# A one-core kernel for local attention and two feed-forward blocks: a new price list for its instruction scheduler, a cheaper mask table, and P·V of two quads in one run

## The chip, the core and the metric

The kernel runs on one NeuronCore of a Trainium2 chip (trn2). A core has five engines with a queue of instructions each: TensorE (PE in the profile, its weight loads PEld), VectorE (DVE), ScalarE (ACT), GpSimd (POOL) and SyncE (SP, which here only issues transfers). Each engine runs its own queue in order, and semaphores hold an instruction back until what it needs is there. PE writes its results to PSUM, which has 8 banks of 128 x 512 fp32 words; all else lies in SBUF. The metric is the device time of one execution in microseconds, the median of several.

## The reference, cut to what matters

```python
# q, k, v: (2, 8, 768, 64) fp32; n_global = 8, n_local = 96
scores = (q @ k.T) / sqrt(64)
keep   = (key < n_global) | ((rel >= 0) & (rel < n_local))      # rel = query - key
dist   = where(global and not local, n_local, abs(rel))
scores = where(keep, scores - slope[head] * dist, -1e9)         # slope[h] = 2 ** -(h + 1)
a      = exp(scores - max) / (sum + 1e-9)
x      = (a @ v) as 1536 tokens x 512
h = x @ w_in        # (512 x 2048)
x = where(h >= 1, h, where(h <= -1, 0, (h + 1) ** 2 / 4)) @ w_out
h = x @ w_in2
out = maximum(0.01 * h, h) @ w_out2                             # 1536 x 512
```

The four weight matrices come as 64-bit floats.

## The kernel before, in words

All products but the transposes and P·V are made in fp32r: each operand is split into a high part and a low rest, and three products (high x high, high x low, low x high) are added up in PSUM.

**Attention.** The 1536 queries are 12 tiles of 128 (`Tt`, `t` its place in its batch of 6), the heads two quads of four, so there are 24 quads (`quad`). A quad sees its own 128 keys and the 128 before them, whose first 32 columns are overwritten by the batch's first 32 keys. Its steps are: load K and Q (`ld`, SP); four transposes into one bank (`tr`, L559, PE); high and low parts of both (`ev_hi`, `ev_lo`, by ACT or DVE); twelve score matmuls (`s_mm`, L591, PE), which use 64 rows of the array each, two at a time; a DVE operation that adds the mask table `b8` and takes the row maximum (`mx`, L600); the exponential with its sum (`ex`, L609, ACT); reciprocal (`rs`, DVE); normalisation (`nm`, L622 on DVE or L624 on POOL); eight transposes of P into two banks (`p_tr`, L633, PE); their evacuation into a buffer `pT` (`p_ev`, ACT or DVE), of which there are two; eight matmuls by V (`x_mm`, L646, PE; sixteen rows in the trace), which use 64 columns of the array each; high and low parts of the result into `x`.

**The mask table.** `b8` has 8 heads x 512 columns. It is made in the first microseconds: POOL writes distances (`c_iota`), DVE or POOL cuts them off at `n_local` (`c_table`, three operations for each of two stretches of columns, 128 and 384), then each head's slope is multiplied in (`c_heads`, sixteen operations, on DVE, ACT and POOL). `n_local` and `n_global` come by two tiny transfers from SP's queue, and a matmul (L387) spreads them over the partitions.

**Feed-forward.** The first block works on 256 tokens at a time for its first two of 16 hidden chunks (matmuls of 128 x 256, woven into the attention), and on 512 at a time for the rest (`hid` L727, `mm` L789, 128 x 512). The second block makes seven products for two groups of 512 tokens instead of eight (`two`: L921, L988, L1003). Each weight chunk of 128 x 512 (64 of them) is loaded as 64-bit words (SP) and turned to fp32 high and low parts in eight steps on ACT, DVE and POOL (`job`: L438 to L465). The last step adds PSUM to `part` and sends it out (L846, L849).

**The order** on every engine is worked out at build time by `Schedule.run`: a list scheduler that goes through the program in modelled time. Each operation has a cost for each engine that may run it and a priority, which is a due time from the tables at L1064 to L1073. An engine that falls free takes the ready operation with the lowest priority whose buffers (rings of tiles: banks, `pT`, `raw` and so on) are free. A consumer on another engine is ready `HOP` = 200 ns after its producer's end. VectorE operations that read no PSUM and POOL operations are not placed at the same modelled time. While the first four quads are not through, PE runs a dummy matmul (L369) wherever the model has it idle.

```python
same = [u for u in o.users if not o.tail and len(u.costs) == 1 and e in u.costs]
heapq.heappush(events, (end, k, e, same))
heapq.heappush(events, (end + o.tail + (0 if e == NONE else self.HOP), k + 0.5, e, (o, [...])))
```

Of the kernel before, what the change touches and what calls it, by code (L numbers as in the profile page):

```python
# [8 lines left out]
F32 = mybir.dt.float32  # L9
# [8 lines left out]
P = 128  # L18
G = 32
# [13 lines left out]
KDN, VDN, QTN, SMN, PTN, GN, RAWN, WDN, WRN = 3, 3, 3, 3, 2, 4, 4, 2, 2  # L33
# [18 lines left out]
class Op:  # L52
    __slots__ = ("costs", "fn", "prio", "takes", "gives", "waits", "users", "at", "done", "tail", "ps")


class Schedule:

    HOP = 200  # L60

    SLOW = 7000.0
# [7 lines left out]
    def add(self, costs, fn, prio, after=(), takes=(), gives=(), tail=0.0, ps=False):  # L70
# [4 lines left out]
        o.costs, o.fn, o.prio, o.gives, o.tail, o.ps = costs, fn, prio, gives, tail, ps  # L75
# [11 lines left out]
    def run(self):  # L87
        ready = [[] for _ in range(6)]
        events = []
        n = 0  # L90
        now = 0.0
        busy = [0.0] * 6

        held = 0.0
        left = len(self.ops)

        def enter(o):
            nonlocal n
            for e in o.costs:
                heapq.heappush(ready[e], (o.prio, n, o))  # L100
                n += 1

# [3 lines left out]
        k = 0  # L106
        while left:
            started = True
            while started:
                started = False  # L110
                for e in range(6):
                    if busy[e] > now:
                        continue
                    kept = []
                    got = None
                    while ready[e]:
                        x = heapq.heappop(ready[e])
                        o = x[2]
                        if o.done is not None:
                            continue  # L120
                        if e == DVE and not o.ps and busy[POOL] > now or e == POOL and held > now:
                            kept.append(x)
                            if len(kept) > 40:
                                break
                            continue
                        if all(len(s.ring.free) > y for s, y in o.takes):
                            got = o
                            break
                        kept.append(x)
                        if len(kept) > 40:  # L130
                            break
                    for x in kept:
                        heapq.heappush(ready[e], x)
                    if got is None:
                        if e == PE and self.fill and self.fill[0].done is not None and self.fill[0].done <= now:
                            self.fill[1]()
                            busy[e] = now + FILLN / (1.2 if now < self.SLOW else 2.4)
                            k += 1
                            heapq.heappush(events, (busy[e], k, e, None))
                        continue  # L140
                    started = True
                    o = got
                    for s, _ in o.takes:
                        s.tile = s.ring.free.pop(0)
                    end = now + o.costs[e] * (2 if e == PE and now < self.SLOW else 1)
                    o.done = end
                    o.at = now
                    busy[e] = end
# [4 lines left out]
                    k += 1  # L153

                    same = [u for u in o.users if not o.tail and len(u.costs) == 1 and e in u.costs]
                    heapq.heappush(events, (end, k, e, same))
                    heapq.heappush(events, (end + o.tail + (0 if e == NONE else self.HOP), k + 0.5, e, (o, [u for u in o.users if u not in same])))
# [3 lines left out]
            now = events[0][0]  # L161
            while events and events[0][0] <= now:
                users = heapq.heappop(events)[3]
                if users is None:
                    continue
                if isinstance(users, tuple):
                    o, users = users
                    for s in o.gives:
                        s.ring.free.append(s.tile)
                for u in users:  # L170
# [1046 lines left out]
```

## Time and profile before

| | us |
|---|---|
| median of 3 runs | 617.87 (617.7 to 618.28) |
| the profiled execution, first to last instruction (span) | 615.8 |
| PE busy in it | 607.2 (99%) |
| DVE, ACT, POOL busy | 474.5, 354.4, 204.9 |
| last matmul starts | 608.4 (its group of three) |

The profiled execution's span is 615.8 us, 2.0 us under the median of the runs; the runs also hold what lies before the first and behind the last instruction. PE's rows give a start that is recorded and an end that is modelled, and each matmul's row overlaps the next, so what a run of matmuls takes is read from its start to the start of the run behind it. Dummy matmuls count as busy.

### The profile page before, as it was taken

The numbers are of one execution on the slowest core, as the hardware profiler recorded it, in microseconds if no ns is written. First come the engines' busy times: TensorE is split into PE (matmuls) and PEld (weight loads), VectorE is DVE, ScalarE is ACT, GpSimd is POOL, SyncE is SP. The second block draws the span as 40 slices with busy tenths as digits, with TensorE's granted clock in tenths as the row PEclk, the third lists the DMA queues.
The fourth block names the chain that finished last, engine by engine and source line by source line (L and its number), as shares of the span: only waits on it lengthen the run. The fifth ranks groups of instructions, "written<-read, shape, count | busy, mean of one in ns | idle before, by whom it ended". The sixth has DMA issues, their size and how long they took to land.

```text
span 615.8 us, 9602 instructions
## 1 busy us (share of the span) xinstructions
PE 607.2 (99%) x3408; PEld 507.2 (82%) x3408; DVE 474.5 (77%) x1036; ACT 354.4 (58%) x762; POOL 204.9 (33%) x248
## 2 busy tenths in 40 slices
PE   8999999999999999999999999999999999999995
PEld 7879888898888888888888888888888888888884
DVE  6999999989983779923469998736988966988563
ACT  6999889767764446734436476524465634464300
POOL 3556576632320102300104152202646422546200
PEclk9999999999999999999999999999999999999998
DMA  9846433124330314300002013200232320220014
GB/s 192 207 104 177 136 89 87 53 65 158 121 110 28 102 35 136 107 32 1 0 11 92 5 65 101 72 1 1 68 106 68 101 69 1 68 70 1 2 65 146
DMA packets 61809, 46.98 MB, mean 76 GB/s; under 512 B 39608, under 2 KB 56248, under 8 KB 61752
## 3 DMA queue, kind: packets, MB, share of 16 engines
q1 hardware_dynamic: 61752, 46.28, 25.8%
q8 instruction: 29, 0.48, 0.4%
q14 instruction: 28, 0.23, 0.1%
HBM read 43.12 MB, written 3.15 MB: 75 GB/s over the span
## 4 chain that ended last, share of the span: by engine, by line


## 5 line engine op out<-in xcount | busy, mean ns | idle before, releaser
L789 PE MATMUL bank<-g,w 128*128 128x512 f32 (+1 forms) x648 | 141.3, 367 | 0.0
L727 PE MATMUL bank<-x,w 128*128 128x512 f32 (+1 forms) x648 | 140.6, 367 | 0.0
L789 PEld LDWEIGHTS bank<-g,w 128*128 128x128 f32 x648 | 112.6, 188 | 20.5 <-issue 0.7
L727 PEld LDWEIGHTS bank<-x,w 128*128 128x128 f32 x648 | 112.3, 188 | 20.1 <-issue 0.3
L828 DVE TENSOR_TENSOR part<-bank,part 128x512 f32<-128x512 f32 x96 | 63.6, 686 | 27.3 <-PE bank L1003 23.2
L1003 PE MATMUL bank<-w,g 128*128 128x512 f32 x312 | 80.9, 389 | 0.0
L1003 PE MATMUL bank<-w,w 128*128 128x512 f32 x264 | 70.1, 389 | 0.0
L459 POOL TENSOR_TENSOR wd<-wd,wr 128x512 int32<-128x512 int32 x33 | 44.9, 1362 | 72.0 <-DVE wd L452 67.6
L1003 PEld LDWEIGHTS bank<-w,g 128*128 128x128 f32 x312 | 58.6, 188 | 12.2
L220 ACT CAST g<-t 128x512 fp32r<-128x512 f32 (+1 forms) x73 | 42.6, 585 | 41.2 <-PE bank L789 20.6
L220 ACT CAST w<-wd 128x512 fp32r<-128x512 f32 x61 | 37.8, 620 | 45.0 <-DVE wd L459 13.4
L734 ACT ACTIVATE t<-bank,half 128x512 f32<-128x512 f32 (+1 forms) x54 | 34.3, 638 | 47.1 <-PE bank L727 42.6
L228 POOL TENSOR_TENSOR w<-wd,w 128x512 fp32r<-128x512 f32 x32 | 42.5, 1332 | 52.3 <-ACT w L220 48.3
L1003 PEld LDWEIGHTS bank<-w,w 128*128 128x128 f32 x264 | 49.6, 188 | 10.3
L749 DVE SCALAR_TENSOR_TENSOR t<-bank,t 128x512 f32<-128x512 f32 (+1 forms) x54 | 33.9, 628 | 28.7 <-ACT t L742 28.1
L444 POOL TENSOR_SCALAR wd<-wd 128x512 f32<-128x512 f32 x26 | 17.5, 673 | 111.5 <-ACT wd L438 101.1
L452 DVE SCALAR_TENSOR_TENSOR wd<-raw,wd 128x512 int32<-128x512 int32 x64 | 49.5, 774 | 1.7
L226 DVE TENSOR_TENSOR g<-t,g 128x512 fp32r<-128x512 f32 (+1 forms) x54 | 37.0, 692 | 16.5 <-ACT g L220 15.8
L456 ACT ACTIVATE wr<-raw 128x512 int32<-128x512 uint32 x64 | 42.4, 670 | 10.5 <-DVE wd L459 10.1
L921 PE MATMUL bank<-x,w 128*128 128x512 f32 x192 | 47.8, 390 | 0.0
L609 ACT ACTIVATE sm<-sm,st 128x256 f32<-128x256 f32 (+1 forms) x96 | 46.2, 490 | 1.9 <-DVE st L600 1.9
L988 PE MATMUL bank<-x,w 128*128 128x512 f32 x192 | 45.1, 389 | 0.0
(116 smaller groups left out, 953.7 us busy)
## 6 DMA issues: line engine op xcount, KB each, us to landing
raw<-in_moe_w_in_dram SPq DMA_DIRECT2D x32, 512.0 KB, 3.8
raw<-in_moe_w_out_dram SPq DMA_DIRECT2D x32, 512.0 KB, 3.4
kd<-in_k_dram SPq DMA_DIRECT2D x24, 128.0 KB, 3.0
qd<-in_q_dram SPq DMA_DIRECT2D x24, 128.0 KB, 3.5
vd<-in_v_dram SPq DMA_DIRECT2D x12, 256.0 KB, 3.2
out_dram<-part SPq DMA_DIRECT2D x11, 256.0 KB, 3.2
out_dram<-part SPq DMA_DIRECT2D x2, 128.0 KB, 3.4
vg<-in_v_dram SPq DMA_DIRECT2D x2, 64.0 KB, 3.9
```

What stands on the lines that cost most here:

```text
L220: A.copy(out=out_, in_=in_)
L228: GP.tensor_tensor(out=out_, in0=a, in1=b, op=ALU.subtract)
L452: V.scalar_tensor_tensor(out=Dd.tile, in0=hl()[0], scalar=-0x40000000, in1=Dd.tile, op0=ALU.bitwise_and, op1=ALU.bitwise_or)
L456: A.activation(out=Rr.tile, in_=hl()[1], func=AF.Copy, scale=2.0 ** -29)
L459: (V if e == DVE else GP).tensor_tensor(out=Dd.tile, in0=Dd.tile, in1=Rr.tile, op=ALU.add)
L609: A.activation(out=Sm.tile[:, a, 0:W], in_=Sm.tile[:, a, 0:W], func=AF.Exp, scale=-1.0, bias=St.tile[:, 0, a:a + 1], accum_out=St.tile[:, ...
L727: T.matmul(out=Hb.tile[:, 0:n], lhsT=wi.tile[:, a, kk * P:(kk + 1) * P], rhs=x[r][:, b, kk, c0:c0 + n], start=(kk == 0 and a + b == 0), st ...
L789: T.matmul(out=o[:, z * n:(z + 1) * n], lhsT=wo.tile[:, a, cc * P:(cc + 1) * P], rhs=Gt.tile[:, b, 0:n], start=st, stop=sp_)
L828: V.tensor_tensor(out=part[r][sl], in0=ac(), in1=part[r][sl], op=ALU.add)
L921: T.matmul(out=bank.tile, lhsT=w.tile[:, a, (2 * z + kk) * P:(2 * z + kk + 1) * P], rhs=xx()[:, b, kx + kk, :], start=st and kk == 0 and a ...
L988: T.matmul(out=Hb.tile, lhsT=w.tile[:, a, kk * P:(kk + 1) * P], rhs=x[2][:, b, kk, :], start=(kk == 0 and a + b == 0), stop=(kk == KD - 1 ...
L1003: T.matmul(out=Bo.tile, lhsT=Gt[z, r].tile[:, b, cb * P:(cb + 1) * P], rhs=wo[z].tile[:, a, :], start=(z == 0 and a + b == 0), stop=(z == ...
```

## The change

1. **The scheduler's model.** The single `HOP` becomes a latency by the producer's engine, one table for consumers on PE (`LAG_PE`) and one for the others (`LAG`). PE's operations have a kind: plain, transpose, scores (64 rows), P·V (64 columns). A table `TURNS` prices the change from one kind to another, and PE looks through up to twelve ready operations for the lowest sum of priority and ten times that price. Transfers have a size; the model lets them queue behind each other at 4.6 ns for each KB, and an issue is priced at 0.5 us. K and Q of a quad are two operations instead of one. Operations that may run on several engines can have a later due time on one of them (`LATE`). All due times have new values; the old ones stay for the fallback that the shown inputs don't take.
2. **The mask.** `c_far` (POOL, while `n_local` is on its way) makes `far` = distance x 1e30. `c_table` then needs one DVE operation for each stretch: max(far − (n_local − 0.5) x 1e30, distance). The table `tab` has one entry for each pair of heads (4 x 512 columns), eight operations instead of sixteen. The odd head's slope is half of the even head's, so `ev_hi` and `ev_lo` multiply Q by `sc` (1 on the first 64 partitions, 2 on the others), and `mx` scales that head by half as much.
3. **P·V in one run.** `quad` is a generator now, and from tile 3 on (`X2` = 3) the P·V matmuls of a tile's two quads are one operation, made when the second quad comes to it. There is still `PTN` = 2. The rings `sm` and `st` have 4 places instead of 3.
4. **The two tiny transfers** of `n_local` and `n_global` go out from ACT's queue, ahead of its table load.

```diff
+PLAIN, TURN, ROWS, COLS = range(4)
+TURNS = ((0, 50, 125, 165), (-82, 0, 92, 92), (185, 185, 0, 185), (153, 153, 120, 53))
+LAG = (200, 140, 120, 80, 50, 0)
+LAG_PE = (0, 285, 240, 300, 100, 0)
+LOOK = 12
+PER_KB = 4.6
+STICK = 10.0
...
-    HOP = 200
...
+        def pick(e):
...
+                if e != PE:
+                    got = x
+                    break
+                c = x[0] + STICK * TURNS[mode][o.mode]
+                if got is None or c < best:
+                    got, best = x, c
+                seen += 1
+                if seen >= LOOK:
+                    break
...
+                    c = o.costs[e]
+                    if e == PE:
+                        c = c * (2 if now < SLOW else 1) + TURNS[mode][o.mode]
+                        mode = o.mode
+                    end = land = now + c
+                    if o.kb:
+                        busy[e] = max(end, landed - BACKLOG)
+                        land = landed = max(busy[e] + o.tail, landed + o.kb * PER_KB)
...
+    def c_far(e, c0, c1):
+        GP.tensor_scalar(out=far[:, c0:c1], in0=rel[:, c0:c1], scalar1=1.0e30, scalar2=0.0, op0=ALU.mult, op1=ALU.add)
+
     def c_n(e):
         V.tensor_copy(out=n_f, in_=Nb.tile[:, 0:2])
+        V.tensor_scalar(out=cut, in0=Nb.tile[:, 0:1], scalar1=-0.5, scalar2=1.0e30, op0=ALU.add, op1=ALU.mult)
...
     def c_table(e, c0, c1):
-        E = V if e == DVE else GP
-        r, u = rel[:, c0:c1], far[:, c0:c1]
-        E.tensor_scalar(out=u, in0=r, scalar1=nl, scalar2=1.0e30, op0=ALU.is_ge, op1=ALU.mult)
-        E.tensor_tensor(out=r, in0=r, in1=u, op=ALU.add)
+        r = rel[:, c0:c1]
+        V.scalar_tensor_tensor(out=r, in0=far[:, c0:c1], scalar=cut, in1=r, op0=ALU.subtract, op1=ALU.max)
...
-        for h in range(h0, h0 + 4):
-            o, r, f = b8[:, h, c0:c1], rel[:, c0:c1], -8.0 * 2.0 ** (-8.0 * (h + 1) / H)
+        for p in (p0, p0 + 1):
+            o, r, f = tab[:, p, c0:c1], rel[:, c0:c1], -8.0 * 2.0 ** (-8.0 * (2 * p + 1) / H)
...
-                nc.sync.dma_start(out=n_w[0:1, :, z], in_=a.bitcast(I32))
+                A.dma_start(out=n_w[0:1, :, z], in_=a.bitcast(I32))
...
         def ev_lo(e):
-            for z in range(2):
-                sub(e, at(z, 1), two(b1.tile[:, z * 2 * P:(z + 1) * 2 * P]), at(z, 0).bitcast(F32))
+            kk, qq = two(b1.tile[:, 0:2 * P]), two(b1.tile[:, 2 * P:4 * P])
+            sub(e, at(0, 1), kk, at(0, 0).bitcast(F32))
+            V.scalar_tensor_tensor(out=at(1, 1), in0=qq, scalar=sc, in1=at(1, 0).bitcast(F32), op0=ALU.mult, op1=ALU.subtract)
...
-        ob = add({PE: 436 * nb + 100}, x_mm, d + DUE["xmm"], oa + vx, takes=[b4, h4], gives=[Pt] + vs_)
-        vx_op[i] = ob
+        heldx[i] = x_mm, oa + vx, [b4, h4], [Pt] + vs_
+        if Tt >= X2 and not last:
+            yield
+        if Tt < X2 or last:
+            of = [i - 1, i] if Tt >= X2 else [i]
+            ob = add({PE: 436 * nb * len(of)}, lambda e, of=of: [heldx[z][0](e) for z in of], t_att[of[0]] + due_["xmm"], sum((heldx[z][1] for z in of), []),
+                     takes=sum((heldx[z][2] for z in of), []), gives=sum((heldx[z][3] for z in of), []), mode=COLS)
...
+S2, X2 = 99, 3
```

PE's queue, tile 3: the P·V matmuls of its two quads (`pT` is the evacuated P, `vd` are V's rows, `kd` and `qd` the loaded K and Q of a later quad). Before:

```order
L646 MATMUL bank_72<-pT_128,vd_117 64x128 x2
L646 MATMUL bank_72<-pT_128,vd_115 64x128 x2
L646 MATMUL bank_72<-pT_128,vd_117 64x128 x2
L646 MATMUL bank_72<-pT_128,vd_115 64x128 x2
L559 MATMUL bank_73<-ident,kd_111 128x128 x2
L559 MATMUL bank_73<-ident,qd_114 128x128 x2
L646 MATMUL bank_76<-pT_129,vd_117 64x128 x2
L646 MATMUL bank_76<-pT_129,vd_115 64x128 x2
L646 MATMUL bank_76<-pT_129,vd_117 64x128 x2
L646 MATMUL bank_76<-pT_129,vd_115 64x128 x2
```

And now:

```order
L694 MATMUL bank_76<-pT_130,vd_117 64x128 x2
L694 MATMUL bank_76<-pT_130,vd_115 64x128 x2
L694 MATMUL bank_76<-pT_130,vd_117 64x128 x2
L694 MATMUL bank_76<-pT_130,vd_115 64x128 x2
L694 MATMUL bank_77<-pT_131,vd_117 64x128 x2
L694 MATMUL bank_77<-pT_131,vd_115 64x128 x2
L694 MATMUL bank_77<-pT_131,vd_117 64x128 x2
L694 MATMUL bank_77<-pT_131,vd_115 64x128 x2
L602 MATMUL bank_73<-ident,kd_109 128x128 x2
L602 MATMUL bank_73<-ident,qd_112 128x128 x2
```

The transposes of K and Q no longer part the two quads. Over the whole order, PE comes to score matmuls 24 times before and 19 times now, and to P·V 23 times before and 15 times now. Its dummy matmuls are 94 before and 84 now; 41 of them stood ahead of the first score matmul, now 33. Ahead of the last P·V stood 228 matmuls of 128 x 256 and 24 of 128 x 512; now 216 and none. All other matmuls are the same in number and shape.

DVE's queue, from the copy of `n_local` and `n_global` out of PSUM (`n_f`) to the first quad's low parts (`ks`, `qt`); `t_98` holds the distances. Before:

```order
L343 COPY n_f<-bank_72 128x2
L344 TENSOR_SCALAR gl<-gl,n_f 128x32
L345 TENSOR_SCALAR gl<-gl,n_f 128x32
L350 TENSOR_SCALAR t_99<-t_98,n_f 128x128
L351 TENSOR_TENSOR t_98<-t_98,t_99 128x128
L353 TENSOR_TENSOR t_98<-t_98,gl 128x32
L350 TENSOR_SCALAR t_99<-t_98,n_f 128x384
L351 TENSOR_TENSOR t_98<-t_98,t_99 128x384
L355 COPY t_98<-gl 128x32
L226 TENSOR_TENSOR ks<-bank_71,ks 128x2x128
L226 TENSOR_TENSOR qt_119<-bank_71,qt_119 128x2x128
```

And now:

```order
L381 COPY n_f<-bank_71 128x2
L382 TENSOR_SCALAR cut<-bank_71 128x1
L383 TENSOR_SCALAR gl<-gl,n_f 128x32
L384 TENSOR_SCALAR gl<-gl,n_f 128x32
L388 SCALAR_TENSOR_TENSOR t_98<-t_99,cut,t_98 128x128
L390 TENSOR_TENSOR t_98<-t_98,gl 128x32
L388 SCALAR_TENSOR_TENSOR t_98<-t_99,cut,t_98 128x384
L392 COPY t_98<-gl 128x32
L259 TENSOR_TENSOR ks<-bank_72,ks 128x2x128
L619 SCALAR_TENSOR_TENSOR qt_119<-bank_72,sc,qt_119 128x2x128
```

Two operations are gone and a one-column one has come. Of the operations that write the table, four stood on DVE, eight on ACT and four on POOL; now none, four and four. Ahead of DVE's last attention operation stood 450 operations, now 434; among them 13 evacuations of P of 128 x 512, now 7.

SP's queue from its start. Before:

```order
L656 DMA kd_109<-in_k_dram 128x4x64
L656 DMA qd_112<-in_q_dram 128x4x64
L384 DMA n_w<-in_n_local_dram 1x2x1
L384 DMA n_w<-in_n_global_dram 1x2x1
L656 DMA kd_110<-in_k_dram 128x4x64
L656 DMA qd_113<-in_q_dram 128x4x64
L656 DMA kd_111<-in_k_dram 128x4x64
```

And now:

```order
L703 DMA kd_109<-in_k_dram 128x4x64
L703 DMA qd_112<-in_q_dram 128x4x64
L703 DMA kd_110<-in_k_dram 128x4x64
L703 DMA qd_113<-in_q_dram 128x4x64
L470 DMA raw_78<-in_moe_w_in_dram 128x4x256
L703 DMA kd_111<-in_k_dram 128x4x64
L703 DMA qd_114<-in_q_dram 128x4x64
```

The second quad's K and Q come up by the two tiny transfers, and a weight chunk stands ahead of the third quad's.

## Rows read from the trace of the kernel before

**Rows 1.** The page's head and its busy times.

```profile
span 615.8 us, 9602 instructions
PE 607.2 (99%) x3408; PEld 507.2 (82%) x3408; DVE 474.5 (77%) x1036; ACT 354.4 (58%) x762; POOL 204.9 (33%) x248
```

**Rows 2.** Four stretches: busy us (instructions) of PE, PEld, DVE, ACT, POOL; clock; DMA share, GB/s.

```profile
0.00:4.42 4.42, 3.36 (x18) 2.45 (x19) 0.41 (x6) 1.28 (x1) 2.49 (x15) 1.00 0.28 63
4.42:28.60 24.18, 23.67 (x240) 19.63 (x239) 22.39 (x107) 21.46 (x78) 8.99 (x22) 1.00 0.97 225
28.60:128.00 99.40, 99.05 (x1007) 86.15 (x1005) 93.53 (x339) 88.20 (x275) 59.81 (x97) 1.00 0.41 104
128.00:600.00 472.00, 471.93 (x2111) 391.70 (x2110) 352.87 (x580) 243.45 (x409) 133.61 (x116) 1.00 0.19 60
```

**Rows 3.** The dummy matmuls (L369) alone: PE busy, PEld busy.

```profile
4.42:28.60 24.18, 10.38 (x78) 7.44 (x77) 1.00 0.97 225
```

**Rows 4.** Timeline of PE in the attention: start us, us, instruction, how many.

```profile
42.43 0.97 PE L591 MATMUL bank<-ks,qt 64*128 64x256 f32 x12
43.33 0.65 PE L633 MATMUL bank<-ident,sm 128*128 128x128 f32 x4
43.92 1.09 PE L646 MATMUL bank<-pT,vd 128*64 128x128 f32 x16
44.94 0.44 PE L559 MATMUL bank<-ident,kd 128*128 128x128 f32 x2
...
47.95 0.38 PE L559 MATMUL bank<-ident,kd 128*128 128x128 f32 x2
...
48.39 0.60 PE L633 MATMUL bank<-ident,sm 128*128 128x128 f32 x4
```

**Rows 5.** Timeline of PE where two P·V runs follow each other, and behind.

```profile
87.81 1.97 PE L646 MATMUL bank<-pT,vd 128*64 128x128 f32 x32
89.71 0.98 PE L591 MATMUL bank<-ks,qt 64*128 64x256 f32 x12
...
91.03 1.67 PE L727 MATMUL bank<-x,w 128*128 128x256 f32 x12
92.53 0.60 PE L633 MATMUL bank<-ident,sm 128*128 128x128 f32 x4
```

**Rows 6.** Waits of PE's weight loads: us in total, times, longest us.

```profile
PEld bank L633 <- DVE sm L622: 1.2, 4, 0.4
...
PEld bank L559 <- DMA qd<-in_q_dram: 0.8, 1, 0.8
```

**Rows 7.** Timeline of PE at the only gap behind the attention.

```profile
357.31 1.29 PE L789 MATMUL bank<-g,w 128*128 128x512 f32 x5
358.68 1.20 PE L921 MATMUL bank<-xt,w 128*128 128x512 f32 x4
```

**Rows 8.** Timeline of DVE and POOL, and PE's loads, at a wait of PE.

```profile
36.31 1.72 DVE L622 TENSOR_SCALAR sm<-sm,st 128x256 f32<-128x256 f32 x4
...
36.78 0.61 POOL L444 TENSOR_SCALAR wd<-wd 128x512 f32<-128x512 f32 x1 [2.00 <-ACT wd L438]
37.37 1.00 POOL L624 TENSOR_SCALAR sm<-sm,st 128x256 f32<-128x256 f32 x2
37.59 0.20 PEld L633 LDWEIGHTS bank<-ident,sm 128*128 128x128 f32 x2 [0.44 <-DVE sm L622]
...
39.82 0.59 DVE L622 TENSOR_SCALAR sm<-sm,st 128x256 f32<-128x256 f32 x2
```

**Rows 9.** DVE's groups for the table and the evacuated P: busy us, mean ns.

```profile
L222 DVE COPY pT<-bank 128x512 f32<-128x512 f32 x13 | 8.8, 686 | 1.8 <-PE bank L633 1.8
L364 DVE TENSOR_SCALAR b<-t 128x384 f32<-128x384 f32 x4 | 1.2, 356 | 0.0
L351 DVE TENSOR_TENSOR t<-t,t 128x384 f32<-128x384 f32 x1 | 0.6, 558 | 0.0
L350 DVE TENSOR_SCALAR t<-t,n_f 128x384 f32<-128x384 f32 x1 | 0.4, 416 | 0.0
```

More of the change, by code (lines that the diff above doesn't have):

```diff
@@ L99, in enter, with event @@
             for e in o.costs:
-                heapq.heappush(ready[e], (o.prio, n, o))
+                heapq.heappush(ready[e], (o.prio + o.late.get(e, 0.0), n, o))
                 n += 1
+        def event(at, e, o, kind):
+            nonlocal k
+            k += 1
+            heapq.heappush(events, (at, k, e, o, kind))
+        def pick(e):
+            kept = []
+            got = None
+            best = 0.0
+            seen = 0
+            while ready[e]:
+                x = heapq.heappop(ready[e])
+                o = x[2]
+                if o.done is not None:
+                    continue
+                kept.append(x)
+                if len(kept) > 40:
+                    break
+                if e == DVE and not o.ps and busy[POOL] > now or e == POOL and held > now:
+                    continue
+                if not all(len(s.ring.free) > y for s, y in o.takes):
+                    continue
+                if e != PE:
[6 more added lines that the diff above has]
+                if seen >= LOOK:
+                    break
+            for x in kept:
+                if x is not got:
+                    heapq.heappush(ready[e], x)
+            return got and got[2]
         for o in self.ops:
@@ L105, in run @@
                 enter(o)
-        k = 0
         while left:
@@ L113, in run @@
                         continue
[L114 to L131, printed above, removed]
@@ L152, in run @@
                     left -= 1
[L153 to L157, printed above, removed]
+                    event(end, e, None, 0)
+                    event(land + LAG[e], e, o, 1)
+                    event(land + LAG_PE[e], e, o, 2)
             if not events:
@@ L215, in emit, with LATE @@
     sch = Schedule()
+    def LATE(kind):
+        return {e: due_[kind + "@" + n] for e, n in ((ACT, "A"), (DVE, "V")) if kind + "@" + n in due_}
     add = sch.add
@@ L666, in quad @@
         elif t > 1:
[L667 removed]
+            kv_op[i] = add(fc, first, d + due_["kg"], [s_op[i - NQ], kv_op[i - NQ]], late=LATE("kg"))
         else:
             kv_op[i] = kv_op[i - NQ]
[L670 to L672 removed]
+        held[i] = s_mm, [ol, kv_op[i] if t > 1 else None], b2 + h2 + [Sm, St], [Qt]
@@ new lines, in quad @@
+        if Tt >= S2 and not last:
+            yield
+        if Tt < S2 or last:
+            of = [i - 1, i] if Tt >= S2 else [i]
+            o4 = add({PE: 720 * len(of)}, lambda e, of=of: [held[z][0](e) for z in of], t_att[of[0]] + due_["s"], sum((held[z][1] for z in of), []),
+                     takes=sum((held[z][2] for z in of), []), gives=sum((held[z][3] for z in of), []), mode=ROWS)
+            for z in of:
+                s_op[z] = o4
+            if Tt >= S2:
+                yield
@@ L673, in quad @@
+        o4 = s_op[i]
         o6 = []
         for z in range(2):
-            o5 = add({DVE: 2 * (dve(W) + 10)}, mx(z), d + DUE["mx"] + z, [o4, o_tb[1 if t else 0][pq]], gives=[b2[z], h2[z]], ps=True)
-            o6.append(add({ACT: 2 * (180 + act(W, False))}, ex(z), d + DUE["ex"] + z, [o5]))
-        o7 = add({DVE: 278}, rs, d + DUE["rs"], o6)
-        opt = add({NONE: 0}, lambda e: None, d - 4300, [o7], takes=[Pt])
-        nms = [add({POOL: 2 * (pool_ts(W) + 83), DVE: 2 * (dve(W, True) + 62)}, nm(y), d + DUE["nm"] + y, [o7]) for y in range(2)]
@@ L680, in quad @@
-        o9 = [add({PE: 110 * 2 * nb}, p_tr(y), d + DUE["ptr"] + y, [nms[y], opt], takes=[b3[y], h3[y]])
+            o5 = add({DVE: 2 * (dve(W) + 10)}, mx(z), d + due_["mx"] + z, [o4, o_tb[1 if t else 0][pq]], gives=[b2[z], h2[z]], ps=True)
+            o6.append(add({ACT: 2 * (180 + act(W, False))}, ex(z), d + due_["ex"] + z, [o5]))
+        o7 = add({DVE: 278}, rs, d + due_["rs"], o6)
+        opt = opts[i] = add({NONE: 0}, lambda e: None, d - 4300, [o7, opts.get(i - 1)], takes=[Pt])
+        nms = [add({POOL: 2 * (pool_ts(W) + 83), DVE: 2 * (dve(W, True) + 62)}, nm(y), d + due_["nm"] + y, [o7], late=LATE("nm")) for y in range(2)]
```

221 lines of the change are left out of this document (117 added, 104 removed).

## The prediction

> **What bounds the kernel now.** I began with the head of the page: a span of 615.8 us in which PE is busy for 607.2 [rows 1]. Matmul rows overlap and dummies count, so this alone does not make PE the bound. The stretches of the span say more [rows 2]. From 128 to 600 us PE is busy for 471.93 of 472.00 us while DVE has work for 352.87: behind the attention PE is the only bound, and the one gap that I find there is at 358 us, where five matmuls that take 0.227 each at their usual distance (1.13) are followed only after 1.37 [rows 7], a loss of 0.2. From 28.6 to 128 us PE is busy for 99.05 of 99.40, but DVE for 93.53 and ACT for 88.20: three engines are nearly full there. From 4.42 to 28.6 PE looks just as full, but 10.38 of its 24.18 us are dummies [rows 3], so here it waits for others, and the dummies show where.
>
> So the time is what PE does, one thing after another, from its first real matmul (4.42 us, where I cut the first stretch) to the last one, and a tail that both kernels share: in the order the last 30 rows of PE and DVE are of the same kinds. A change to this kernel counts as far as it takes something out of PE's queue, or a wait from between its instructions.
>
> **What changes of kind cost.** In the timeline of PE, starts tell the price [rows 4]. Twelve score matmuls take 43.33 − 42.43 = 0.90; four transposes between scores and P·V 43.92 − 43.33 = 0.59; sixteen P·V rows 44.94 − 43.92 = 1.02; four transposes among transposes 48.39 − 47.95 = 0.44. Going into a run of 64 rows or columns and coming out of one thus adds 0.15 to the transposes at its two sides. Where two P·V runs follow each other, 32 rows take 89.71 − 87.81 = 1.90 [rows 5], so the second sixteen cost 0.88 and the way out of P·V 0.14. For scores no such row stands; six pairs at the distance of a dense 128 x 256 matmul (92.53 − 91.03 = 1.50 for twelve, 0.125 each [rows 5]) would take 0.75, which leaves 0.15 for the way out. Its bounds are 0 (if a pair takes 0.15) and 0.18.
>
> PE comes to P·V 8 times less and to scores 5 times less. Each spared visit saves the way in and out at the neighbours, 0.15, and the way out in the run itself: 8 x 0.29 + 5 x 0.30 = 3.8 us. Merged runs alone, without anything saved at the neighbours, would give 8 x 0.14 = 1.1 us; with visits that also leave straight for one another, and not by way of a transpose, it may be 4.3. I take 4.0.
>
> **Dummies.** Ten fewer. 78 of them make 10.38 us [rows 3], 0.133 each, and less where they lie back to back; I take 0.11 each, 1.1 us. The lower bound is 0: a dummy that is gone can leave a plain wait in its place. The upper one is 1.3. What makes room is the front of the queue. Before, the third and fourth loads were issued behind the two tiny ones, and PE waited 0.8 us for them once [rows 6]; now they go out third and fourth, and this wait should end. On DVE the table's two long operations of 0.416 and 0.558 become one of about the second's size, and the four of 0.356 that wrote heads are gone [rows 9]: with the short stretch some 1.7 us less on DVE, in the very microseconds when PE runs dummies. ACT drops four operations there. None of this adds a second time: it is what lets the 41 dummies ahead of the first scores become 33. The `sc` multiply rides on operations that stood there already, with a price between nothing and about 0.1 us for each of 24 quads on ACT or DVE; neither is PE.
>
> **Waits.** Before, PE waited for DVE's normalisation four times, 1.2 us in all, and 0.8 us for the load [rows 6], and 0.2 at 358 us: 2.2 us. The load's part goes. What happens to the others is the open question, and the reason that I don't forecast the whole sum. Ahead of the end of the attention DVE is busy for 0.41 + 22.39 + 93.53 = 116.3 us [rows 2]. By the order 16 operations fewer stand there now; at six P evacuations of 0.686 [rows 9], the table's 1.7 and small pieces both ways it is some 7 us less, about 109. But PE has dense matmuls moved behind the attention, 12 x 0.125 + 24 x 0.227 = 6.9 us, which cost nothing in the sum and everything in cover: the attention should end at 128 − 4.0 − 1.1 − 6.9 = 116 us. From 4.4 us on DVE would then be busy for 109 of 112 us, 97%, where it was 116 of 124, 94%. The last evacuations may trail PE by some two or three microseconds, since dense matmuls follow, so 95% is nearer. Bounds on the waits: below, 0; above, all of DVE's idle time until 128 us (124 − 116 = 8 us) seen by PE. I take 2.6: the 1.2 of the four waits doubled, since the room that DVE leaves about halves (8 us of idle time before, some 4 now), and the 0.2. That is 0.4 more than before.
>
> **Sum.** Against the profiled execution's own span: 615.8 − 4.0 − 1.1 + 0.4 = 611.1 us. The runs' median lies 2.1 us above that span, so 613.2 us; the change is −4.7 us or −0.8%. A measurement of this kernel can tell about 0.2% (1.2 us) from no change: 616.6 to 619.1 counts as the same.
>
> **Rivals.**
>
> *The fuller DVE gives it back.* One of PE's four waits can be taken apart [rows 8]: four normalisations on DVE took 1.72 together from 36.31 on while POOL ran two operations, where two of them at 39.82 took 0.59, and PE's next loads stood still for 0.44. [...] The scheduler keeps the two apart in its modelled time, before and now, but real time drifts. With DVE's order 95 to 97% full a lost piece is not made up. If DVE keeps the 8 us of idle time that it had until 128 us, its last attention operation ends at 4.4 + 109 + 8 = 121.4, where PE's plan has it at 116 + 1.4: 4 us late, and 5.1 − 4 leaves 1.1 us, 616.8 us. For it: rows 2 and 8. Against it: much of that idle time was DVE waiting for PE, and would vanish.
>
> *The merged run holds both buffers.* There are two `pT`, and both are taken until a merged P·V ends, so evacuation and P·V of neighbouring quads no longer overlap; P·V then waits for the last transposes' evacuation, 0.69 on DVE [rows 9], behind what stands in its queue. In the order at least twelve dense matmuls (1.50 [rows 5]) or two score runs (0.75 to 0.90 each [rows 4]) stand between, so it should be covered. If ACT and DVE are late by another microsecond at each of the nine merged runs, it costs 9 us, and 617.9 − 5.1 + 9 = 621.8. It turns the sign from (5.1 + 1.2) / 9 = 0.7 us for each run.
>
> *All waits go.* The latencies by engine are right, and the new order leaves no wait: 617.9 − 5.1 − 2.2 = 610.6 us.
>
> *The first part hardly counts.* The ways out are hidden behind weight loads that PE would wait for anyway, only 1.1 for merged runs and little of the dummies come through: 617.9 − 1.5 = 616.4, at the edge of the same.
>
> **Chances.** The forecast (611 to 615) 0.52; all waits go (under 611) 0.13; DVE gives it back (615 to 618.5) 0.18; the small gain 0.07; the held buffers or another new wait (over 619) 0.10. Leaving out half of the best case and the worst one, eight in ten lie between 610.4 and 617.4. Of the two middle rivals about a third falls within 0.2%: faster 0.81, same 0.09, slower 0.10.
>
> **What would show it.** Dummies: the group of L410, 84 rows, and 33 of them ahead of the first score matmul. Kinds: the timeline of PE shows L694 in runs of 32 rows with 1.9 us to the next start, and the last one ends near 116 us. Waits: in the list of PE's weight loads the load of Q no longer stands and the sum over DVE and ACT is near 2 us. DVE: busy about 109 us until its last attention operation. Dense stage: unchanged but for its start, 0.227 for each matmul, with no gap of more than some tenths. I am wrong if PE's waits ahead of its transposes of P or ahead of P·V add up to 5 us or more, or if the dense stage starves for weights, which would show as gaps ahead of L727 and L789.

## The result, and the profile after

The changed kernel takes 611.87 us (median of 4 runs, 611.8 to 612.29) against 617.87: a ratio of 0.9902, with a 95% interval of 0.9888 to 0.9916. That is 6.0 us less where 4.7 were forecast, and inside the range. The profiled execution has a span of 610.0 us against 615.8, so again some 1.9 us lie around the span and the 5.8 can be looked for inside it.

The page's head and its busy times answer to [rows 1]; PE has ten dummies fewer and is as full as before:

```profile
span 610.0 us, 9623 instructions
PE 601.5 (99%) x3398; PEld 506.4 (83%) x3398; DVE 471.4 (77%) x1044; ACT 351.6 (58%) x753; POOL 193.4 (32%) x244
```

The stretches, with the attention cut at 118 us now (length; busy us and instructions of PE, PEld, DVE, ACT, POOL; clock; DMA share, GB/s), answer to [rows 2]:

```profile
4.42:28.60 24.18, 24.09 (x245) 19.63 (x243) 23.11 (x108) 21.74 (x75) 13.03 (x29) 1.00 0.98 221
28.60:118.00 89.40, 89.39 (x974) 82.24 (x972) 87.06 (x325) 86.27 (x271) 51.31 (x91) 1.00 0.49 115
118.00:600.00 482.00, 481.23 (x2156) 399.64 (x2155) 358.55 (x602) 242.34 (x408) 125.79 (x107) 1.00 0.19 61
```

Three engines stand side by side at 96 to 100% of the 89.40 us, and PE still has almost no idle time. Behind the attention PE lacks 0.77 of 482 us, where it lacked 0.07 of 472.

The timeline of PE (start us, us, instruction, how many) answers to [rows 4, 5]. Runs of 24 scores and of 32 P·V rows stand next to each other, with no transposes between them, and the last P·V run of the attention ends over 13 us earlier (dense matmuls moved behind it as well):

```profile
49.95 1.70 PE L639 MATMUL bank<-ks,qt 64*128 64x256 f32 x24
51.58 1.97 PE L694 MATMUL bank<-pT,vd 128*64 128x128 f32 x32
53.48 0.44 PE L602 MATMUL bank<-ident,kd 128*128 128x128 f32 x2
...
112.75 1.97 PE L694 MATMUL bank<-pT,vd 128*64 128x128 f32 x32
114.64 0.74 PE L796 MATMUL bank<-x,w 128*128 128x512 f32 x2
```

From start to start the 24 scores take 1.63; twice the 0.90 of a run of twelve [rows 4] would be 1.80, so the way out of scores costs 0.17. The 32 rows of P·V take 1.90, as in [rows 5].

The waits of PE's weight loads (us in total, times, longest) answer to [rows 6]:

```profile
PEld bank L990 <- DVE bank L1035: 1.2, 1, 1.2
...
PEld bank L428 <- DVE n_g L432: 0.6, 1, 0.6
PEld bank L694 <- DVE st L648: 0.5, 3, 0.2
```

The four waits for DVE's normalisation and the one for the load of Q are gone; the largest is a new one, in the second block. The wait for `n_g` (0.6) is new too: it stands ahead of the matmul that spreads `n_local` and `n_global` (the count). The timeline of all engines shows how the largest comes about:

```profile
520.86 1.54 POOL L261 TENSOR_TENSOR g<-t,g 128x512 fp32r<-128x512 f32 x1 [1.41 <-ACT g L253]
...
521.17 1.78 DVE L502 CUSTOM_DVE_ANT_0 wd<-wd,wr 128x1024 uint16<-128x1024 uint16 x1
...
522.36 1.74 POOL L261 TENSOR_TENSOR w<-t,w 128x512 fp32r<-128x512 f32 x1
...
522.87 1.52 DVE L491 TENSOR_SCALAR wd<-wd 128x512 int32<-128x512 int32 x1
...
524.31 0.68 DVE L897 TENSOR_TENSOR part<-bank,part 128x512 f32<-128x512 f32 x1
524.91 0.68 DVE L1035 TENSOR_TENSOR bank<-bank,s 128x512 f32<-128x512 f32 x1
...
525.65 1.66 PE L990 MATMUL bank<-xt,w 128*128 128x512 f32 x6 [0.77 <-DVE bank L1035]
```

Two DVE operations in a row run long beside POOL: L502, 0.68 in its 31 other runs, takes 1.78, and the bit mask L491, about 0.42 in 54 of its 64 runs and 0.9 or more in nine, takes 1.52 and ends 0.3 behind POOL's end. The sum that PE waits for (L1035) is queued two places behind the mask. Operations like these are what the rival "the fuller DVE gives it back" starts from [rows 8], here in a place that the prediction had not in view.

**Where the 5.8 us went.** PE's last matmul, the third of its group, starts at 603.08 instead of 608.83, 5.75 earlier. The last groups, before and now:

```profile
608.38 0.84 PE L1003 MATMUL bank<-w,g 128*128 128x512 f32 x3
```

```profile
602.62 0.84 PE L1072 MATMUL bank<-w,g 128*128 128x512 f32 x3
```

Ten dummies fewer, at 0.11 from start to start where they lie back to back, make 1.1. Gaps between PE's instructions, read from start to start in both traces, sum to some 1.9 before (0.68 for the load of Q at 6.0 to 6.7, 0.84 for normalisations at 36.4 to 38.1, 0.34 at 358.5 to 359.0) and 1.6 after (0.30 ahead of the matmul that spreads the count, 0.27 inside a run of scores at 80.0, 1.04 at 524.5 to 526.0), which makes 0.3. The rest, 4.4, is what PE does between kinds: 15 visits to P·V for 23, 19 to scores for 24, and 36 to transposes for 51, counted in the order. Added up from start to start and without these gaps, PE's transposes take 2.7 us less than before, P·V 1.4 and scores 0.7 less, and dummies, but for their number, 0.5 more, in part since scores now start behind one more often.

### The profile page after: what moved, and what is told of

It reads as the page before. It is cut to its first block, busy times and chain, and to the rows that moved or that the text cites. A ratio compares the mean times of both kernels' runs of the same rounds, so it can differ in the third digit from the quotient of the medians.

```text
span 610.0 us, 9623 instructions
## 1 busy us (share of the span) xinstructions
PE 601.5 (99%) x3398; PEld 506.4 (83%) x3398; DVE 471.4 (77%) x1044; ACT 351.6 (58%) x753; POOL 193.4 (32%) x244
## 4 chain that ended last, share of the span: by engine, by line
## 5 line engine op out<-in xcount | busy, mean ns | idle before, releaser
L502 POOL TENSOR_TENSOR wd<-wd,wr 128x512 int32<-128x512 int32 x32 | 45.8, 1434 | 111.5 <-DVE wd L495 62.9
L253 ACT CAST g<-t 128x512 fp32r<-128x512 f32 (+1 forms) x67 | 39.5, 590 | 56.6 <-PE bank L858 30.5
L253 ACT CAST w<-wd 128x512 fp32r<-128x512 f32 x64 | 39.6, 621 | 27.0 <-DVE wd L502 9.2
L259 DVE TENSOR_TENSOR g<-t,g 128x512 fp32r<-128x512 f32 (+1 forms) x58 | 41.4, 718 | 15.1 <-ACT g L253 14.8
L495 DVE SCALAR_TENSOR_TENSOR wd<-raw,wd 128x512 int32<-128x512 int32 x64 | 47.6, 754 | 0.5
L672 POOL TENSOR_SCALAR sm<-sm,st 128x256 f32<-128x256 f32 (+1 forms) x78 | 37.8, 501 | 26.4 <-DVE st L663 21.2
L259 DVE TENSOR_TENSOR w<-wd,w 128x512 fp32r<-128x512 f32 x55 | 37.6, 695 | 7.7 <-ACT w L253 6.9
```

Source lines behind the costliest of these rows:

```text
L253: A.copy(out=out_, in_=in_)
L259: V.tensor_tensor(out=out_, in0=a, in1=b, op=ALU.subtract)
L495: V.scalar_tensor_tensor(out=Dd.tile, in0=hl()[0], scalar=-0x40000000, in1=Dd.tile, op0=ALU.bitwise_and, op1=ALU.bitwise_or)
L502: (V if e == DVE else GP).tensor_tensor(out=Dd.tile, in0=Dd.tile, in1=Rr.tile, op=ALU.add)
```

## The experiments

Theory: the attention is bound by PE's queue, and the gain is visits and dummies that left it, with waits that did not grow. Rivals: the ways between kinds are hidden anyway; DVE sets the pace; or the gain sits in one part (mask, early loads) or in the table of due times and not in the visits. Of the kernels below the first group keeps the changed order and edits single instructions; the second lets the scheduler plan anew.

**What a visit costs.** Two kernels with the same 48 dummies, in and behind the runs of P·V:

```diff
# e1_split: at the end of each half of x_mm
+                T.matmul(out=b4.tile[:, FILLN:2 * FILLN], lhsT=zero[:, 0:P], rhs=zero, start=True, stop=True)
# e2_behind: the same matmul, 2 * len(of) times, behind the whole (merged) operation
```

> The changed kernel in its own order, with a plain dummy matmul of 256 columns put behind each half of a quad's P by V: 48 dummies, 33 of them inside a run of P by V that stood together before, so 33 more visits to P by V. The changed kernel's median is 611.9. Theory kinds (PE's queue is the bound in the attention, a visit costs 0.14 on the way out and up to 0.15 on the way in): 48 x 0.11 = 5.3 for the dummies and 33 x 0.29 = 9.6 for the visits, 626.8; with the way out alone 33 x 0.14 = 4.6, 621.8. Rival, ways in and out are hidden behind weight loads: the dummies alone, 617.2. Rival, DVE sets the pace of the attention: PE's added work goes into its waits, under 614.

> The same 48 dummies, but all of them behind the run of P by V that they belong to, so that no run is cut and no visit is added. Theory kinds: the dummies alone, 48 x 0.11 = 5.3, so 617.2, and 5 to 10 us less than the kernel with the cut runs; a little more if the next kind is entered worse from a dummy than from P by V. Rival, the ways are hidden: the same time as the cut runs. Rival, DVE sets the pace: under 614.

Measured: 624.6 us (ratio 1.012, 1.0102 to 1.0138) with the runs cut, and 615.91 (0.9973, 0.9962 to 0.9984) with the dummies behind. The 48 dummies cost 4.0, under the 5.3 expected, and the 33 cuts 8.7, so 0.26 each, between the 0.14 and the 0.29 of the two forecasts. In the rows the dummies themselves take 5.2; the transposes and scores behind them take 1.1 less than in the changed kernel. The timeline of PE of the cut kernel:

```profile
46.52 0.66 PE L694 MATMUL bank<-pT,vd 128*64 128x128 f32 x8
47.11 0.28 PE L696 MATMUL bank<-zero 128*128 128x256 bf16 x1
47.33 0.66 PE L694 MATMUL bank<-pT,vd 128*64 128x128 f32 x8
```

and of the other:

```profile
45.08 1.97 PE L694 MATMUL bank<-pT,vd 128*64 128x128 f32 x32
46.98 0.61 PE L756 MATMUL bank<-zero 128*128 128x256 bf16 x4
47.43 0.38 PE L602 MATMUL bank<-ident,kd 128*128 128x128 f32 x2
```

Eight rows and a dummy take 0.81 when cut; uncut, eight inner rows are 0.44 and a dummy behind 0.11. The difference, 0.26, is the price in the rows, and it comes through whole in the time. "The ways are hidden" is out, and so is a DVE that alone sets the pace. This is the price for P·V; for scores no run adds a visit by itself.

**Dummies.** Only the first 17 are issued:

```diff
+        fills.append(0)
+        if len(fills) <= 17:
             T.matmul(out=still.tile[:, 0:FILLN], lhsT=zero[:, 0:P], rhs=zero[:, 0:FILLN], start=True, stop=True)
```

> The changed kernel in its own order, with only the first 17 dummies issued; the other 67 are left out. If the dummies stood where PE would wait anyway, the time stays: 611.4 to 612.4, with plain waits where they were; if a dummy's end is often behind the arrival of the work, by half a dummy for each of the 22 stretches of them, 22 x 0.05 = 1.1 less, 610.8. If each dummy was pure load on PE's queue, 67 x 0.11 = 7.4 less, 604.5. If the granted clock falls in the gaps, more than 613, and the windows up to 28.6 us show it.

Measured: 612.14 us (0.9906, 0.989 to 0.9921), as with dummies. The clock did fall, as the last branch has it, but the time stayed below its 613. (The stretches of dummies are 13 in the rows, 12 of them left out here, not 22.) The mean granted clock of the stretch from 4.42 us is 0.79, where it is 1.00 in the changed kernel:

```profile
4.42:28.60 24.18, 22.26 (x173) 16.68 (x171) 21.89 (x103) 20.62 (x70) 12.82 (x29) 0.79 0.94 215
```

The dummies are no load worth removing: without them PE waits in their place and runs part of the stretch slower (the granted clock is 0.50 from 7.6 to 17.8 us; two transposes at 11.66 take 0.43 from start to start, against 0.22 at 5.41 in the changed kernel). How much of the 7.4 us of dummies each of the two takes, the run does not tell. Ten fewer are a sign that work came sooner, not a gain by themselves.

**The mask.** The table by the two operations of before, and each head written twice; the order is kept:

```diff
-        V.scalar_tensor_tensor(out=r, in0=far[:, c0:c1], scalar=cut, in1=r, op0=ALU.subtract, op1=ALU.max)
+        V.tensor_scalar(out=u, in0=r, scalar1=nl, scalar2=1.0e30, op0=ALU.is_ge, op1=ALU.mult)
+        V.tensor_tensor(out=r, in0=r, in1=u, op=ALU.add)
```

> The changed kernel in its own order, but the distance table is made by the two operations of before (compare and scale, then add) on DVE instead of the one, and each head's table is written twice, as many writes as before. On DVE that is some 0.3 + 0.4 us more ahead of the first evacuations of K and Q, on ACT 1.4 and on POOL 2.1 us more. Theory start (what DVE does ahead of the first scores is on the path): first scores later by 0.5 to 0.8 us than 7.91, and the whole kernel by as much, 612.4 to 612.7. Rival, the dummies that follow take it up: within 0.2 of 611.9. If the head tables of POOL and ACT come late for the first masks it is up to 2 us, 613.9.

Measured: 612.74 us (0.992, 0.9907 to 0.9934), 0.9 more. The intervals of the two kernels overlap, and the row decides: the first run of scores, 0.99 long in the changed kernel, waits inside for 0.66. DVE comes to the first low parts that much later, at 7.96 instead of 7.29:

```profile
7.91 1.65 PE L640 MATMUL bank<-ks,qt 64*128 64x256 f32 x12
```

```profile
7.96 0.41 DVE L259 TENSOR_TENSOR ks<-bank,ks 128x256 fp32r<-128x256 f32 x1
```

Another 0.23 is lost inside the third run of scores, at 14. The last PE instruction starts 0.9 later too, at 603.98: what stands ahead of the first scores comes through to the end.

**The early loads.** The two small loads on SP's queue, between the first and the second pair of K and Q, order kept:

```diff
-                A.dma_start(out=n_w[0:1, :, z], in_=a.bitcast(I32))
+                nc.sync.dma_start(out=n_w[0:1, :, z], in_=a.bitcast(I32))
```

> The changed kernel in its own order, with only the two small loads moved: back on SP's queue, behind the first loads of K and Q and ahead of the second ones, as before. Undone with a new plan this made 6 us. Theory, the new plan was what cost: in the old order the small loads land later by two issues of a big load (about 0.5 each in rows of SP's queue) and the second pair by two issues of the small ones, so the first scores come at most some 1.2 us later than 7.91: 612.4 to 613.2 against 611.9. Rival, the transfers are worth what the new plan showed: 615 or more. If DVE's work covers it: 611.6 to 612.2.

Measured: 611.92 us (0.9902, 0.9887 to 0.9918), no change, where the theory had 0.5 to 1.3 more. DVE, which has no pause between 5.2 and 9.3 us, reaches the first masked sum no later. Two rows of DVE, of the changed kernel:

```profile
7.29 0.42 DVE L259 TENSOR_TENSOR ks<-bank,ks 128x256 fp32r<-128x256 f32 x1
...
9.47 0.28 DVE L648 CUSTOM_DVE_ANT_0 sm<-bank,tab 128x128 f32<-128x128 f32 x1
```

and of this one:

```profile
7.08 0.42 DVE L259 TENSOR_TENSOR ks<-bank,ks 128x256 fp32r<-128x256 f32 x1
...
9.39 0.29 DVE L651 CUSTOM_DVE_ANT_0 sm<-bank,tab 128x128 f32<-128x128 f32 x1
```

PE's first scores start at 8.27 instead of 7.91, and in this profile PE stays 0.35 behind to its last matmul (603.42). That need not be the loads: the record of the granted clock begins at 5.92 us here and at 4.86 there, and in both profiles dummies start 0.21 apart ahead of it and 0.11 behind it. The two small loads themselves come later from ACT's queue, which the change had not in view: DVE takes up their words at 4.74 in the changed kernel, at 4.32 here and at 4.33 in the kernel before.

**How much room DVE has.** One small operation more for each quad:

```diff
             V.reciprocal(out=St.tile[:, 2], in_=St.tile[:, 2])
+            V.scalar_tensor_tensor(out=spare, in0=spare, scalar=1.0, in1=spare, op0=ALU.mult, op1=ALU.max)
```

> The changed kernel in its own order, with one more DVE operation of 128x64 on a spare tile for each of 24 quads, put behind the reciprocal of the row sums, 0.13 to 0.2 us each: 3.1 to 4.8 us more on DVE, and nothing more on PE. PE alone bounds the attention and DVE has room: under 612.3. DVE is as full as PE (87.06 of 89.40 us busy from 28.6 to 118, and 23.11 of 24.18 ahead of it): what goes beyond its 2.3 us of idle time there comes through, 612.7 to 614.4. The whole comes through if DVE's idle time cannot be used: up to 616.7.

Measured: 616.06 us (0.9963, 0.995 to 0.9977), 4.2 more, where only the last branch reaches so far. The group of the added operation, and the longest wait of PE's loads:

```profile
L666 DVE SCALAR_TENSOR_TENSOR spare<-spare 128x64 f32<-128x64 f32 x24 | 5.7, 239 | 0.0
```

```profile
PEld bank L861 <- DVE st L650: 1.5, 1, 1.5
```

22 of the 24 take 0.19 to 0.20; one takes 1.22 at 92.94 beside a POOL operation of 1.26, and PE's wait of 1.5 follows it. Part of the price is thus this one long operation: in modelled time the scheduler keeps DVE operations that read no PSUM apart from POOL's, and it knew nothing of the added one. From start to start PE's last matmul is 3.8 later: 0.4 is lost before 5.9 us, ahead of the first added operation (12.6 us), 1.5 at this wait, 0.3 behind the attention, and 1.6 in small pieces between. So what is added to PE comes through, and what is added to DVE comes through in part: without the long one, 1.6 us for 4.5 us of its time, near the 2.2 that go beyond the 2.3 us of idle time.

**The new wait.** The bit mask is issued behind the sum, nothing else (v_cc); and with the five small operations of the test for the wide case moved behind the attention as well (v_best):

```diff
+            if (c, o) == (29, 1):
+                behind.append(go)
+            else:
+                go()
...
+                V.tensor_tensor(out=Bc.tile, in0=Bb.tile, in1=S5.tile, op=ALU.add)
+                if j == 6:
+                    behind.pop()()
```

> The changed kernel in its own order but for one operation: the bit mask of 0.42 on DVE, which took 1.52 beside a POOL operation at 522.9 us and stood ahead of the sum that PE waits for, is issued behind that sum. Theory, a DVE operation held up beside POOL makes the one wait of 1.04 in the dense stage: the wait goes, 610.9. Rival, PE's wait is due to DVE's queue as a whole and the next operation is late by as much: 611.6 to 612.0. If the mask is now late for its weights, over 612.2.

> The changed kernel in its own order with two moves on DVE: the bit mask behind the sum that PE waited 1.04 for, as run already by itself, and the five small operations that test for the wide case (0.56 us ahead of the table) moved behind the attention. Theory: 0.7 to 1.0 from the first, up to 0.3 from the second where DVE's work ahead of the first scores is on the path: 610.6 to 611.2 against 611.9. Rival for the second, DVE waits there for the matmul that spreads the count anyway: no more than the first by itself brought, 611.2.

Measured: 611.36 us (0.9896, 0.9881 to 0.991) and 611.51 (0.9895, 0.988 to 0.991). In the first the wait is gone and the mask takes its usual time:

```profile
524.38 0.70 DVE L1041 TENSOR_TENSOR bank<-bank,s 128x512 f32<-128x512 f32 x1
...
524.99 0.41 DVE L492 TENSOR_SCALAR wd<-wd 128x512 int32<-128x512 int32 x1
...
525.47 1.30 PE L995 MATMUL bank<-xt,w 128*128 128x512 f32 x5
```

So the rows show it as the theory has it: with the mask of 1.52 no longer ahead of the sum, the wait of 1.04 is gone. The half microsecond in the medians is as expected in sign, but the intervals overlap that of the changed kernel: no measurable gain over it. In the profile the front takes part of the gain back. PE runs the same instructions in the same order in both kernels, but in the profile of v_cc the record of the granted clock begins at 6.57 instead of 4.86 us. The same two transposes, in the changed kernel and in v_cc:

```profile
5.41 0.38 PE L602 MATMUL bank<-ident,kd 128*128 128x128 f32 x2
```

```profile
5.80 0.63 PE L607 MATMUL bank<-ident,kd 128*128 128x128 f32 x2
```

PE is 0.77 behind by 6 us; with the wait gone it is 0.29 ahead behind 526, so the wait is worth 1.05. In v_best, where that record begins at 4.08, PE goes from 0.09 ahead to 1.12, and the gain is lost again at the end, in the issue of the last transfer (see the last section). The second move adds nothing: with it PE is 0.09 earlier at the first scores.

**Plans made anew.** Four kernels in which the scheduler orders everything again:

```diff
# m_nomerge
-S2, X2 = 99, 3
+S2, X2 = 99, 99
# m_early
-                A.dma_start(out=n_w[0:1, :, z], in_=a.bitcast(I32))
+                nc.sync.dma_start(out=n_w[0:1, :, z], in_=a.bitcast(I32))
-        o_n = add({ACT: 1000}, c_words, -9.9e9, tail=DLAT, kb=1)
+        o_n = add({SP: 1000}, c_words, -9e9, tail=DLAT, kb=1)
# x_wide
-    due_ = DUE if narrow else WIDE
+    due_ = dict(WIDE, tab=-7.9e9, hd=2000.0, hd1=6000.0)
# c_kb
-PER_KB = 4.6
+PER_KB = 4.7
```

> The changed kernel with only the merging undone: each quad's P by V is an operation of its own again, and the scheduler plans anew. In the order PE then comes to P by V 22 times in place of 15 and to scores 22 times in place of 19; dummies stay at 84. Theory kinds, with 0.26 for a cut of P by V as the two dummy kernels had it, and 0.2 to 0.3 for a visit to scores: 7 x 0.26 + 3 x 0.25 = 2.6, so 614.5 against 611.9. Rival, the merged run makes waits of its own by holding both transposed buffers, which go when it is undone: 611.5 to 613. If single runs also bring new waits: over 615.5.

> The changed kernel with the two small loads of the window and the global count back on SP's queue, behind the loads of K and Q, planned anew: 102 dummies in place of 84 and the same visits to P by V, one fewer to scores. Theory start: what is late there is late to the end, 18 more dummies at 0.11 make 2.0, with the visit 1.7: 613.6, up to 614.5 with waits from an order that the due times were not made for. Rival, the early loads bring nothing, since the long work of DVE sets the first scores: under 612.3.

> The changed kernel with the due times of before in place of its own table, all else as changed: merged P by V, latencies by pair of engines, prices, the one-operation mask, the early loads. In the order P by V is visited 15 times, scores 23 times in place of 19, with 72 dummies in place of 84. If the parts carry the gain and the table only fits them: 4 visits to scores at 0.25 make 1.0, and up to 2 us of waits come on top: 612 to 615. If the table is what removes the waits: over 616, with PE's waits 4 us or more.

> A control: the changed kernel with one number of the planner's model moved by 2 per cent (4.7 in place of 4.6 ns for each KB of a load), nothing else. No operation is added or removed; in the order P by V is visited 15 times and scores 19 times as before the edit, dummies are 93 in place of 84. Theory, the table of due times fits one order and any other order it yields waits: 9 dummies at 0.11 make 1.0, and waits of 1 to 4 us come on top as in the other kernels that were planned anew, 614 to 617. Rival, a new plan by itself is harmless and the loss of the kernel with the small loads on SP's queue was the loads': 611.5 to 613.

Measured: m_nomerge 616.02 us (0.9967, 0.9954 to 0.9981), m_early 617.85 (0.9995, 0.9986 to 1.0004), x_wide 623.54 (1.0095, 1.008 to 1.0111), c_kb 615.83 (0.9967, 0.9956 to 0.9979). m_nomerge and m_early came out above their theories (614.5, and 613.6 to 614.5), x_wide where the table is what removes the waits, and c_kb inside its own. This control decides how to read the others: a number of the planner's model that is off by 2% costs 4.0 us, with the visits to scores and P·V unchanged and nine dummies more. Its waits of PE's loads:

```profile
PEld bank L681 <- POOL sm L672: 1.2, 3, 0.8
...
PEld bank L681 <- POOL ks L255: 0.7, 2, 0.5
```

Normalisations and copies on POOL are late for the transposes of P here; the changed kernel's list has no such wait. So the 6.0 of m_early are the new plan's, not the loads' (the same loads, order kept, cost nothing). Part of them is the clock: in its profile a DVE operation of 128x4 takes 1.26 beside POOL at 59.2, PE idles 1.4 us ahead of 62.2, and behind that the granted clock is 0.50 for a while:

```profile
63.52:66.93 3.41, 3.41 (x20) 2.85 (x20) 2.34 (x11) 3.41 (x14) 1.69 (x4) 0.50 1.09 237
```

The 4.1 of m_nomerge are no clean price of merging either, but its rows part them. PE's last matmul is 4.4 later (607.50). Its first scores are 0.65 later, in a profile whose record of the granted clock begins at 6.67 instead of 4.86. Two new gaps in the second block take 1.0:

```profile
PEld bank L1072 <- DVE part L897: 0.7, 1, 0.7
PEld bank L990 <- ACT bank L253: 0.7, 1, 0.7
```

The other 2.8 lie in the attention, in which no gap of PE is longer than 0.2: they are seven more visits to P·V, three to scores and nine to transposes, close to the 2.6 that the theory had for the first two.

With the due times of before all the other parts together are slower than the kernel before, by 0.95%, and the list of waits shows why:

```profile
PEld bank L681 <- DVE sm L670: 3.4, 8, 1.0
PEld bank L990 <- DVE bank L1038: 2.8, 3, 1.3
PEld bank L639 <- DVE qt L619: 2.0, 3, 1.6
```

One more reading, of the order alone: with the price of kinds in the scheduler's choice set to nothing (`STICK = 0.0` for 10.0) the order is the same in every row of all five engines. Due times in the table are of the order of 100000, and 10 times a price of 185 does not reorder them. So the fewer visits come from the due times and the merging, not from this rule; the prices still count in the modelled time.

## Why the prediction was right

**The bound** held: 33 cuts, 0.26 each and so 8.6 in the rows of PE, came out as 8.7 in the time, and 48 dummies, 5.2 in the rows less 1.1 at their neighbours, as 4.0.

**Kinds**, forecast 4.0 (1.1 to 4.3): the balance above leaves 4.4, a little over the upper bound. The price for a visit to P·V, 0.29 from neighbouring rows, measured 0.26 by itself; for scores the way out, taken as 0.15, is 0.17. Eight visits at 0.26 and five at 0.17 + 0.15 make 3.7. That P·V now follows scores directly spares ways to and from transposes as well, which the bound of 4.3 had in view; no run prices these by themselves.

**Dummies**, forecast 1.1: ten fewer, 84 with 33 ahead of the first scores, make 1.1. The reason given was half right. DVE's shorter table is confirmed (0.9 us when undone, 0.66 of it at DVE's first low parts). The loads in third and fourth place, to which I put down the end of the 0.8 wait, bring nothing: with the small ones in front again the wait for Q is 0.2 and the time is the same. That DVE's queue hides it is likely from its rows, but not shown.

**Waits**, forecast to go from 2.2 to 2.6: this term had the wrong sign. "The 1.2 of the four waits doubled, since the room that DVE leaves about halves" is the step that failed. DVE's room did shrink as worked out (0.43 + 23.11 + 87.06 = 110.6 us until 118, forecast 109), and the added operation shows that it has little left, yet the waits for normalisation vanished and the sum is 1.6 (1.9 before when read from starts in the same way). Less room does not mean more waits where the order places each operation: x_wide, as full (87.01 of the same 89.40), waits 3.4 us for normalisation alone, and c_kb, one number apart, has waits that the changed kernel has not. The waits hang on the fit of the table to the order, and the trace of before does not show that fit. The time lay within the range all the same: the span is 1.1 us under the forecast, for kinds gave 0.4 and waits 0.7 more than forecast, and the second was luck, since the working had them grow.

**Rivals.** "The fuller DVE gives it back" has its case in the dense stage, worth 1.0 and not the 4 of its sum: the mask took 1.1 more than usual beside a POOL operation of 1.74 that had begun 0.5 before it. "The held buffers": no wait ahead of P·V above 0.2 in the changed kernel, so nine merged runs cost nothing there. "All waits go" came as near in time as the forecast (610.6 and 613.2, each 1.3 off), but not in fact, since 1.6 us of waits are left. "The first part hardly counts" is refuted by the cut runs.

What stays open is how the 6.0 us split between merging and the table: neither was undone without a new plan, and every new plan made here cost 4 us or more. The rows of m_nomerge put merging, with the visits that go with it, at some 2.8; this is a reading of one profile and not a run that isolates it.

## What to carry to other kernels

When an order is planned from a table that was fitted to one program, undo a part by moving instructions in the finished order; let the planner run again only with a control beside it, here 4 us for a 2% edit. On an engine that bounds, count changes of kind as work: 0.26 us for a P·V run cut in two, the time of nearly five of its rows. Where three engines are 96 to 100% full, as here, a free slot on the second engine is little cover (24 small operations on DVE made 4.2 us): look at what the operation would run beside. And before two profiles are compared within a microsecond, look where the record of the granted clock begins in each and how far apart dummies start ahead of it.

## What the runs showed of the hardware

DVE operations of three more kinds than those of [rows 8] ran long beside POOL (us for the usual us): the bit mask 1.52 for 0.42, a custom sum 1.78 for 0.68, a 128x64 operation 1.22 for 0.20. With 67 dummies left out, PE stood idle between the first transposes and scores (0.71 us ahead of 7.76), the mean granted clock from 4.42 to 28.60 us was 0.79 instead of 1.00, and the whole took 612.14 us against 611.87. The record of the granted clock begins at another time in each of six profiled executions: at 4.08 us (v_best), 4.16 (before), 4.86 (changed), 5.92 (e_words), 6.57 (v_cc) and 6.67 (m_nomerge). So the 1.00 that [rows 2] has from 0.00 to 4.42 us stands almost wholly for time without a record. In the changed kernel PE runs dummies nearly without a pause from 1.05 us on; they start 0.21 apart until 4.44 and 0.11 apart from 5.20 on. By 6 us v_cc was 0.77 us behind the changed kernel with the same instructions in the same order. And in the profile of v_best the issue of the last output transfer took 2.03 us where it took 0.39 in the changed kernel; the same happened with the added DVE operation (2.09). Its cause stays open. In v_best it hides all that the moves brought: PE's last matmul starts 1.14 earlier than in the changed kernel (601.93), and the span is 0.3 longer.
